# Part A of a gated mix: the order of transpositions, scores and normalizations between the projections

## The chip, the core and the metric

The kernel runs on one core of a Trainium2 chip. The metric is the device time of one execution in microseconds (us). Three executions of the kernel before took 1726.29, 1729.7 and 1736.17 us; the median is 1729.7 us. The profile is of a further execution, which took 1731.97 us.

## What is computed

Two attentions over the same 2048 rows of 640 are mixed by a gate per row. Attention A is recurrent: it goes through 64 segments of 32 rows, and each segment sees 8 memory rows that the segment before made. Attention B (a dilated window of 8 keys) has no recurrence.

```python
for s in range(64):                                   # A: H = 32 heads of Dh = 192, M = 8
    h = concat([mem, x[32*s : 32*s+32]])              # 40 rows
    q, k, v = h @ Wq, h @ Wk, h @ Wv                  # 640 -> 32*192 each
    scores = where(mask, q @ k.T * Dh**-0.5, -1e9)    # per head, 40 x 40
    o = (softmax(scores) @ v) @ Wo                    # 32*192 -> 640
    mem, out_a[s] = o[:8], o[8:]
g = sigmoid((x * gate_w).sum(-1))
return g * a + (1 - g) * b
```

## The kernel before, in words

Part B and a prepass come first (the first 380 us). The prepass also projects the last 8 rows of every segment's own x, since these need no recurrence, and packs the results in memory (`zpk_dram`), from where each segment loads its share: `load_z` (L709, keys and queries, 192 KB) and `load_vz` (L714, values, 96 KB). Part A, `part_a` (L684), is a loop over 64 segments. It fills the rest of the time, but for a last stage of some 60 us, `part_z`.

**A segment.** A projection's weights are 4 groups R of 8 heads. `m_qk(i, kcs)` (L725) projects queries (even i) or keys (odd i) of group R = i // 2; `m_v(R)` (L819) projects values. Such a projection has 5 steps kc, and each step has 4 matmuls of 32 weight columns by 384 columns, side by side on the four column strips of TensorE (tile position (0, 32 j)). In the following such four are called a quad, and this way of dividing the array is called the projections' tile mode. `c_qk(i)` (L738) copies the result from PSUM to a staging area of bf16 in SBUF (ScalarE, for i = 7 VectorE). `t_qk(i)` (L745) transposes it by three 128x128 matmuls against the identity into PSUM. `c_t(i)` (L755) copies the transposed rows on VectorE to where scores read them, for queries with a permutation (L758), for keys straight (L762). Scores are `s_a` (L775, the segment's own 32 keys: FULL is two matmuls with 128 rows, HALF two with 64 rows) and `s_b` (L787, the same against the prepass' keys). `e_exp(h)` (L795), four ScalarE activations, `e_mask(h)` (L801, VectorE) and `e_norm(h)` (L806) make the softmax of half h of the heads: two matmuls with a block of ones sum over keys (L810, L811), ScalarE makes the reciprocal by Ln and Exp (L814, L815), VectorE multiplies (L816, L817). `pv_half(h)` (L836) is 48 small matmuls with values, its results are copied (L861), `c_z` (L866) copies 8 more columns, and `o_group` (L884) is the output projection, 4 matmuls each, again in four column strips.

**The order.** Inside `part_a` the instructions of TensorE, ScalarE and VectorE are issued in the order in which the code is written (L907 to L986). The projections are interrupted by transpositions and scores, which use the array with 128 or 64 rows and 128 columns. I call such an interruption an excursion. The order before has five of them that hold transpositions or scores, and one more for `e_norm(1)`:

1. after m_qk(2): t_qk 0 and 1
2. after m_qk(4): t_qk 2 and 3, s_a(0)
3. after m_qk(6): s_a(1, FULL), s_b(0, FULL), t_qk 4 and 5, s_a(1, HALF), s_b(0, HALF)
4. after m_v(0): t_qk 6 and 7, s_a(2, FULL), e_norm(0), s_a(2, HALF)
5. after m_v(1): s_a(3), s_b(1)
6. within m_v(3): e_norm(1)

**Bytes.** Both areas, TZ and ZB, are shared by hand. Staging has two places (`assert i - 2 not in sts`, L740), so c_qk(i) waits until t_qk(i - 2) has read. Each transposition of a projection has a PSUM tile of its own from the pool `psx`, which has two buffers of one PSUM bank.

**Weights.** Of the 80 slices of weights (384 KB each) 66 stay in SBUF and 14 are streamed anew in every segment through five buffers (`wst`). `weights_setup` (L510) picks the 14 at even distances of an assumed timetable, in which `gap` gives the pauses between slices. DMAs for `wst` are issued on SP; those of `load_z`, `load_vz`, the next segment's x (L650), B's result `a4` (L954), the stores of results (L1001) and of the memory rows' part of the attention (L968) are issued on ScalarE's queue, in the order of the code.

Of the kernel before, what the change touches and what calls it, by code (L numbers as in the profile page):

```python
# [10 lines left out]
BF = mybir.dt.bfloat16  # L11
# [16 lines left out]
class _K:  # L28
# [481 lines left out]
    def weights_setup(self):  # L510
        nc, tc = self.nc, self.tc
        keys = self.slice_keys()
        gap = {("q", 0, 0): 300, ("k", 0, 1): 160, ("k", 0, 3): 70, ("k", 1, 0): 450, ("k", 2, 0): 850, ("k", 3, 0): 1050,
               ("v", 1, 0): 1000, ("v", 2, 0): 600, ("v", 3, 0): 570, ("v", 3, 3): 200, ("oa", 6): 1200}
        at, t = {}, 0
        for k in keys:
            t += gap.get(k, 0)
            at[k] = t
            t += 163
        self.stream_keys = set()  # L520
        for i in range(N_STREAM):
# [12 lines left out]
        self.wstream = self.ctx.enter_context(tc.tile_pool(name="wstream", bufs=WBUFS))  # L534
# [149 lines left out]
    def part_a(self):  # L684
# [4 lines left out]
        with ctx:  # L689
            pers = ctx.enter_context(tc.tile_pool(name="a_pers", bufs=1, reuse_waits="tile"))  # L690
            ZB = pers.tile([128, 1536 + 160], BF, name="ZB")
            KV, ZA = self.TZ[:, 0:1536], self.TZ[:, 1920:2528]
            Vz = ZA[:, 224:608]
            QTa = ZB[:, 384:1536].rearrange("p (b r c i) -> p b r c i", b=6, r=2, i=8)
            Es = [z[:, 0:224].rearrange("p (a f) -> p a f", a=2) for z in (ZA, ZB)]
            zst = ZA[:, 32:416]
            oTz = zst.rearrange("p (c q) -> p c q", q=8)
            whi = ZB[:, 768:768 + 640]
            KT = KV[:, 0:768].rearrange("p (c k) -> p c k", k=32)
            V = [KV[:, f0:f0 + 384] for f0 in (0, 768, 384, 1152)]  # L700
            oTxs = [v.rearrange("p (c q) -> p c q", q=32) for v in V]
            a4 = ZB[:, 1536:1696]
            KTz = self.TZ[:, 1536:1920].rearrange("p (c k) -> p c k", k=32)
# [18 lines left out]
            for s in range(nseg):  # L722
# [14 lines left out]

                def c_qk(i):  # L738

                    assert i - 2 not in sts  # L740
                    sts[i] = KV[:, 768 + 384 * (i % 2):1152 + 384 * (i % 2)]
                    cp = nc.vector.tensor_copy if i == 7 else nc.scalar.copy
                    cp(sts[i], pqs[i][:, 0:384])  # L743

                def t_qk(i):  # L745
                    R = i // 2
                    st = sts.pop(i)
                    pT = psx.tile([128, 1024], BF, tag="x", name="ps_qkT")
                    pT = pT[:, 0:384].rearrange("p (t j b i) -> p t j b i", t=3, j=4, i=8)
                    for t in range(3):  # L750
                        nc.tensor.transpose(pT[:, t, :, :, :].rearrange("p j b i -> p (j b i)"),  # L751
                                            st[:, 128 * t:128 * t + 128], self.ident[:])
                    pTs[i] = pT

                def c_t(i):  # L755
                    R, pT = i // 2, pTs.pop(i)
                    if i % 2 == 0:
                        nc.vector.tensor_copy(  # L758
                            q_blocks(R)[:, 1:5, :, :].rearrange("p b c i -> p c b i"),
                            pT.rearrange("p t j b i -> p (t j) b i"))  # L760
                    else:
                        nc.vector.tensor_copy(KV[:, 384 * (R % 2):384 * (R % 2) + 384],  # L762
                                              pT.rearrange("p t j b i -> p (t j b i)"))

                def q_blocks(R):
                    b0 = 1 - R // 2
# [8 lines left out]
                def s_a(R, chunks):  # L775
                    h, r = R // 2, R % 2
                    if h not in pSs:
                        pSs[h] = psS.tile([128, 2, 512], F32, tag="S", name="ps_S")
                    for t, par, k0, k1 in chunks:
                        c = 4 * t  # L780
                        nc.tensor.matmul(grid(h, par)[:, :, 0:80].rearrange("p j (b r i) -> p j b r i", r=2, i=8)[:, :, :, r, :],  # L781
                                         lhsT=KT[k0:k1, 12 * r + c:12 * r + c + 4, :],
                                         rhs=q_blocks(R)[k0:k1, :, c:c + 4, :].rearrange("p b c i -> p c b i"),
                                         start=(r == 0 and t != 1), stop=False, tile_position=(k0, 0),
                                         skip_group_check=True)
# [20 lines left out]
                def e_norm(h):  # L806
                    E = Es[h]
                    EA, EB = E[:, :, 0:80], E[:, :, 80:112]
                    pz = pSs[h][:, 0, 0:160].rearrange("p (a f) -> p a f", a=2)
                    nc.tensor.matmul(pz, lhsT=self.bones[:], rhs=EA, start=True, stop=False, skip_group_check=True)  # L810
                    nc.tensor.matmul(pz[:, :, 0:32], lhsT=self.bones[:], rhs=EB, start=False, stop=True,  # L811
                                     skip_group_check=True)
                    rz = pz
                    nc.scalar.activation(rz, pz, ACT.Ln)  # L814
                    nc.scalar.activation(rz, rz, ACT.Exp, scale=-1.0)  # L815
                    nc.vector.tensor_tensor(out=EA, in0=EA, in1=rz, op=ALU.mult)  # L816
                    nc.vector.tensor_tensor(out=EB, in0=EB, in1=rz[:, :, 0:32], op=ALU.mult)  # L817
# [95 lines left out]
                    tail()  # L913
                m_qk(0, (3, 4)); c_qk(0)
                m_qk(1, (3, 4)); c_qk(1)
                m_qk(2, range(KC))
                t_qk(0); c_t(0); c_qk(2); t_qk(1); c_t(1)
                m_qk(3, range(KC)); c_qk(3)
                if store is not None:
                    store()  # L920
                load_vz(s)
                m_qk(4, range(KC))
                if s == 0:
                    for load in self.last_loads:
                        load()
                t_qk(2); c_t(2); c_qk(4); t_qk(3); c_t(3)
                s_a(0, FULL); s_a(0, HALF)
                m_qk(5, range(KC)); c_qk(5)
                m_qk(6, range(KC))
                s_a(1, FULL); s_b(0, FULL)  # L930
                t_qk(4); c_qk(6); t_qk(5)
                s_a(1, HALF); s_b(0, HALF)
                c_t(4); c_t(5)
                e_exp(0)
                m_qk(7, range(KC)); c_qk(7)
                e_mask(0)
                m_v(0)
                t_qk(6); c_t(6); t_qk(7); c_t(7)
                s_a(2, FULL)
                e_norm(0)  # L940
                s_a(2, HALF)
                c_v(0)
                if s + 1 < nseg:
                    hT_next = self.load_seg(s + 1)
                else:
# [2 lines left out]
                    self.oz_free += [k for k in self.res_tiles if k[0] == "v"]  # L948
                    self.load_oz(0)
                m_v(1); c_v(1)  # L950
                for chunks in (FULL, HALF):
                    s_a(3, chunks)
                    s_b(1, chunks)
                nc.scalar.dma_start(a4[:], self.bsc_dram[32 * s:32 * s + 32, :].rearrange("t (j f) -> j t f", j=4))  # L954
# [162 lines left out]
```

## Time and profile before

| what | before |
|---|---|
| median of 3 runs | 1729.7 us |
| the profiled execution's time | 1731.97 us |
| its span in the profile | 1729.2 us |
| TensorE busy (matmuls; they overlap) | 1636.4 us, 95% |
| ScalarE, VectorE, GpSimd busy | 861.4 (50%), 632.3 (37%), 59.8 us (3%) |
| granted TensorE clock, mean | 0.99 |
| HBM traffic over the span | 275 GB/s |
| period of a segment in part A, mean of the 62 after the first | 20.42 us |
| the shortest period | 19.70 us (nine of the 62 read so) |

The profiled execution's time is 2.8 us over its span: what lies around the span. A period is the time between the first projection matmuls of two consecutive segments, read from the matmuls' starts in the trace. The chain of waits lists, back from the last instruction, what each step waited for; in part A it is nearly all TensorE work, and pieces called "issue" are times in which TensorE waited for nothing that the profile names.

### The profile page before, as it was taken

The numbers are of one execution on the slowest core, as the hardware profiler recorded it, in microseconds if no ns is written. First come the engines' busy times: TensorE is split into PE (matmuls) and PEld (weight loads), VectorE is DVE, ScalarE is ACT, GpSimd is POOL, SyncE is SP. The second block draws the span as 40 slices with busy tenths as digits, with TensorE's granted clock in tenths as the row PEclk, the third lists the DMA queues.
The fourth block names the chain that finished last, engine by engine and source line by source line (L and its number), as shares of the span: only waits on it lengthen the run. The fifth ranks groups of instructions, "written<-read, shape, count | busy, mean of one in ns | idle before, by whom it ended". The sixth has DMA issues, their size and how long they took to land.

```text
span 1729.2 us, 82024 instructions
## 1 busy us (share of the span) xinstructions
PE 1636.4 (95%) x36281; PEld 976.2 (56%) x36281; DVE 632.3 (37%) x2031; ACT 861.4 (50%) x2338; POOL 59.8 (3%) x124
## 2 busy tenths in 40 slices
PE   7887999899999999999999999999999999999989
PEld 4544544355555655555555555556555556555667
DVE  3665333233333333333333333333333333333330
ACT  3887322235555555555555455555555545555550
POOL 2030000000000000000000000000000000000000
PEclk9999899999999999999999999999999999999999
DMA  7898695989999999899888889989899999998991
GB/s 198 202 228 199 226 319 146 273 276 298 294 301 301 299 299 308 294 294 305 298 291 298 281 290 302 301 292 306 299 297 301 297 290 303 305 300 298 310 295 31
DMA packets 299696, 477.46 MB, mean 276 GB/s; under 512 B 100172, under 2 KB 176460, under 8 KB 299340
## 3 DMA queue, kind: packets, MB, share of 16 engines
q1 hardware_dynamic: 200208, 415.76, 74.2%
q10 hardware_dynamic: 99132, 56.46, 11.5%
q8 instruction: 283, 4.64, 1.1%
q14 instruction: 73, 0.60, 0.1%
HBM read 430.40 MB, written 44.48 MB: 275 GB/s over the span
## 4 chain that ended last, share of the span: by engine, by line
PE 85%; DMA 6%; ACT 3%; issue 3%; DVE 1%; ACTq 1%; SPq 1%; DVEq 0%
PE ps_qk L734 25%; PE ps_v L827 13%; PE ps_wo L891 12%; PE ps_pre L603 6%; PE ps_qkT L751 6%; PE ps_S L781 5%; PE ps_oT L850 3%; PE ps_z L1048 3%; PE ps_pre L617 3%; ACT ZB L975 2%; DMA bqkT<-bqk_dram 2%; PE ps_bqk L234 2%; PE ps_mem L901 1%; PE ps_S L790 1%; DMA OT<-bo_dram 1%
## 5 line engine op out<-in xcount | busy, mean ns | idle before, releaser
L743 ACT CAST TZ<-ps_qk 128x384 bf16<-128x384 f32 x448 | 208.3, 479 | 333.5 <-PE ps_qk L734 189.3
L734 PEld LDWEIGHTS <-hT 128*32 128x32 bf16 x10240 | 247.0, 96 | 158.7 <-issue 17.2
L758 DVE COPY ZB<-ps_qkT 128x384 bf16<-128x384 bf16 x256 | 91.6, 358 | 376.8 <-PE ps_qkT L751 210.5
L734 PE MATMUL ps_qk<-wres_q,hT 128*32 128x384 bf16 x4096 | 225.2, 327 | 2.1 <-issue 2.1
L827 PE MATMUL ps_v<-wlate_v,hT 128*32 128x384 bf16 x4096 | 224.0, 328 | 0.0
L734 PE MATMUL ps_qk<-wlate_k,hT 128*32 128x384 bf16 x3328 | 202.7, 328 | 1.8 <-issue 1.8
L891 PEld LDWEIGHTS <-TZ 128*32 128x32 bf16 x6144 | 154.8, 96 | 68.6 <-issue 20.2
L734 PE MATMUL ps_qk<-wst,hT 128*32 128x384 bf16 x1792 | 154.0, 328 | 1.8 <-issue 1.1
L827 PEld LDWEIGHTS <-hT 128*32 128x32 bf16 x5120 | 113.4, 96 | 67.1 <-issue 4.3
L891 PE MATMUL ps_wo<-wlate_oa,TZ 128*32 128x384 bf16 x2560 | 140.1, 327 | 2.9 <-issue 2.2
L781 PE MATMUL ps_S<-ZB,TZ 128*128 128x160 bf16 (+1 forms) x1024 | 136.4, 237 | 0.3 <-DMA ZB<-zpk_dram 0.3
L891 PE MATMUL ps_wo<-wlate_ob,TZ 128*32 128x256 bf16 x2688 | 124.0, 275 | 8.4 <-issue 7.2
L751 PE MATMUL ps_qkT<-ident,TZ 128*128 128x128 bf16 x1536 | 129.7, 220 | 0.4 <-ACT TZ L743 0.3
L751 PEld LDWEIGHTS <-TZ 128*128 128x128 bf16 x1536 | 89.0, 98 | 61.2 <-issue 40.6
L799 ACT ACTIVATE ZB<-ps_S 32x224 bf16<-32x224 f32 x256 | 89.0, 348 | 42.6 <-PE ps_S L790 38.6
L861 DVE CAST TZ<-ps_oT 128x192 bf16<-128x192 f32 x256 | 79.5, 351 | 63.7 <-PE ps_oT L855 63.5
L861 ACT CAST TZ<-ps_oT 128x192 bf16<-128x192 f32 x256 | 69.8, 327 | 58.3 <-PE ps_oT L855 58.3
L781 PEld LDWEIGHTS <-TZ 128*128 128x128 bf16 (+1 forms) x1024 | 58.8, 95 | 67.8 <-issue 40.4
L904 DVE CAST hT<-ps_mem 128x24 bf16<-128x24 f32 x126 | 22.5, 179 | 202.3 <-PE ps_mem L901 202.3
L834 ACT CAST TZ<-ps_v 128x384 bf16<-128x384 f32 x192 | 92.4, 481 | 3.2
L827 PE MATMUL ps_v<-wst,hT 128*32 128x384 bf16 x1024 | 86.7, 329 | 3.6 <-DMA wst<-in_A_Wv_dram 3.6
L799 ACT ACTIVATE TZ<-ps_S 32x224 bf16<-32x224 f32 x256 | 88.8, 347 | 2.3
(137 smaller groups left out, 2229.9 us busy)
## 6 DMA issues: line engine op xcount, KB each, us to landing
wst<-in_A_Wq_dram SPq DMA_DIRECT2D x260, 384.0 KB
wst<-in_A_Wv_dram SPq DMA_DIRECT2D x260, 384.0 KB
wst<-in_A_Wk_dram SPq DMA_DIRECT2D x195, 384.0 KB
wst<-wscr SPq DMA_DIRECT2D x192, 384.0 KB
zpk_dram<-ZS ACTq DMA_DIRECT2D x4, 3072.0 KB
ZB<-zpk_dram ACTq DMA_DIRECT2D x64, 192.0 KB
wres_q<-in_A_Wq_dram SPq DMA_DIRECT2D x16, 384.0 KB
wlate_v<-in_A_Wv_dram SPq DMA_DIRECT2D x16, 384.0 KB
```

What stands on the lines that cost most here:

```text
L603: nc.tensor.matmul(ps[:], lhsT=sls[r][kc][:, c0:c0 + 128], rhs=zTi[:, kc, :], start=(kc == 0), stop=(kc == KC - 1))
L617: mm = nc.tensor.matmul(pss[g][:], lhsT=zTi[:, kc, 128 * st:128 * st + 128], rhs=sls[kc][:, 512 * g:512 * g + 512], start=(kc == 0), stop= ...
L734: nc.tensor.matmul(pq[32 * j:32 * j + 32, 0:384], lhsT=hT[:, kc, :], rhs=sl[:, 384 * j:384 * j + 384], start=(kc == 0), stop=(kc == KC - 1 ...
L743: cp(sts[i], pqs[i][:, 0:384])
L751: nc.tensor.transpose(pT[:, t, :, :, :].rearrange("p j b i -> p (j b i)"), st[:, 128 * t:128 * t + 128], self.ident[:])
L758: nc.vector.tensor_copy(q_blocks(R)[:, 1:5, :, :].rearrange("p b c i -> p c b i"), pT.rearrange("p t j b i -> p (t j) b i"))
L781: nc.tensor.matmul(grid(h, par)[:, :, 0:80].rearrange("p j (b r i) -> p j b r i", r=2, i=8)[:, :, :, r, :], lhsT=KT[k0:k1, 12 * r + c:12 * ...
L799: nc.scalar.activation(E[ps], pSs[h][ps, :, 112 * j:112 * j + 112], ACT.Exp, scale=scale_a)
L827: nc.tensor.matmul(pvs[R][32 * j:32 * j + 32, 0:384], lhsT=hT[:, kc, :], rhs=sl[:, 384 * j:384 * j + 384], start=(kc == 0), stop=(kc == KC ...
L834: cp(V[R], pvs[R][:, 0:384])
L861: cps[j % 2](oTxs[2 * h + j // 2][:, 6 * (j % 2):6 * (j % 2) + 6, :], pos[j][:, 0:240].rearrange("p (c q) -> p c q", q=40)[:, :, 8:40])
L891: nc.tensor.matmul(pso[part][32 * jj:32 * jj + 32, 0:n], lhsT=oTxs[2 * (R // 2) + j // 2][:, 6 * (j % 2) + 3 * (R % 2) + t, :], rhs=o_weig ...
```

## The change

The order within a segment is rewritten so that there are three excursions with transpositions or scores:

1. after two of the five steps of m_qk(4): t_qk 0 to 3, with c_t 0 to 3 between them
2. after m_qk(7): s_a(0, FULL), s_a(1, FULL), s_b(0, FULL), t_qk 4 to 7, then the three HALF pairs; e_exp(0) and c_t 4 to 7 follow
3. after m_v(1): s_a(2, FULL), s_a(3, FULL), s_b(1, FULL), the sums of e_norm(0), then the three HALF pairs

`e_norm` is cut in two: the matmuls stay in `e_norm`, Ln, Exp and the multiplications become `e_recip`. The sums of half 1 are made by 8 matmuls of 32 columns in the projections' tile mode instead of 2 of 128 columns. Staging has four places. Transpositions i and i + 1 share one PSUM tile, half a bank each. The transposed keys of groups 0 and 1 go to places in ZB and TZ that are free at that time (`kt_runs`; those of group 1 in two copies, one of them where `a4` lies), those of groups 2 and 3 over staging places 2 and 3. The store of the last segment's result is issued before m_qk(2) instead of after m_qk(3), and the load of `a4` comes after e_recip(0). m_v(3) is cut 2 + 2 + 1 instead of 3 + 2. `gap` is given anew, which picks four other slices for streaming (k 1 3, q 2 2, q 3 0 and v 0 0 in place of k 1 0, q 2 4, k 2 2 and q 3 4).

```diff
-        gap = {("q", 0, 0): 300, ("k", 0, 1): 160, ("k", 0, 3): 70, ("k", 1, 0): 450, ("k", 2, 0): 850, ("k", 3, 0): 1050,
-               ("v", 1, 0): 1000, ("v", 2, 0): 600, ("v", 3, 0): 570, ("v", 3, 3): 200, ("oa", 6): 1200}
+        gap = {("q", 0, 0): 300, ("k", 0, 1): 160, ("k", 0, 3): 70, ("q", 2, 2): 900, ("v", 0, 0): 1900, ("v", 2, 0): 1100,
+               ("v", 3, 2): 600, ("v", 3, 4): 200, ("oa", 6): 1200}
...
+            kt_runs = lambda R: ([(0, 3, ZB[:, 0:384])], [(0, 2, self.TZ[:, 1920:2176]), (2, 3, ZB[:, 1536:1664])],
+                                 [(0, 3, V[2])], [(0, 3, V[3])])[R]
...
-                    sts[i] = KV[:, 768 + 384 * (i % 2):1152 + 384 * (i % 2)]
+                    sts[i] = V[i % 4]
...
-                    pT = psx.tile([128, 1024], BF, tag="x", name="ps_qkT")
-                    pT = pT[:, 0:384].rearrange("p (t j b i) -> p t j b i", t=3, j=4, i=8)
+                    if i % 2 == 0:
+                        pTs["two"] = psx.tile([128, 2, 512], BF, tag="x", name="ps_qkT")
+                    pT = pTs["two"][:, i % 2, 0:384].rearrange("p (t j b i) -> p t j b i", t=3, j=4, i=8)
...
-                        nc.vector.tensor_copy(KV[:, 384 * (R % 2):384 * (R % 2) + 384],
-                                              pT.rearrange("p t j b i -> p (t j b i)"))
+                        src = pT.rearrange("p t j b i -> p (t j b i)")
+                        for t0, t1, dst in kt_runs(R):
+                            nc.vector.tensor_copy(dst, src[:, 128 * t0:128 * t1])
...
-                    nc.tensor.matmul(pz, lhsT=self.bones[:], rhs=EA, start=True, stop=False, skip_group_check=True)
-                    nc.tensor.matmul(pz[:, :, 0:32], lhsT=self.bones[:], rhs=EB, start=False, stop=True,
-                                     skip_group_check=True)
+                    if h == 0:
+                        nc.tensor.matmul(pz, lhsT=self.bones[:], rhs=EA, start=True, stop=False, skip_group_check=True)
+                        nc.tensor.matmul(pz[:, :, 0:32], lhsT=self.bones[:], rhs=EB, start=False, stop=True,
+                                         skip_group_check=True)
+                    else:
+                        for x, E_x in ((80, EA), (32, EB)):
+                            for j in range(4):
+                                sl = slice(32 * j, 32 * j + 32)
+                                nc.tensor.matmul(pz[sl, :, 0:x], lhsT=self.bones[:, sl], rhs=E_x, start=(x == 80),
+                                                 stop=(x == 32), tile_position=(0, 32 * j), skip_group_check=True)
+
+                def e_recip(h):
...
-                m_qk(2, range(KC))
-                t_qk(0); c_t(0); c_qk(2); t_qk(1); c_t(1)
-                m_qk(3, range(KC)); c_qk(3)
                 if store is not None:
                     store()
+                m_qk(2, range(KC)); c_qk(2)
+                m_qk(3, range(KC)); c_qk(3)
                 load_vz(s)
-                m_qk(4, range(KC))
+                m_qk(4, (0, 1))
+                for i in range(4):
+                    t_qk(i); c_t(i)
+                m_qk(4, (2, 3, 4)); c_qk(4)
+                m_qk(5, range(KC)); c_qk(5)
...
-                t_qk(2); c_t(2); c_qk(4); t_qk(3); c_t(3)
-                s_a(0, FULL); s_a(0, HALF)
-                m_qk(5, range(KC)); c_qk(5)
-                m_qk(6, range(KC))
-                s_a(1, FULL); s_b(0, FULL)
-                t_qk(4); c_qk(6); t_qk(5)
-                s_a(1, HALF); s_b(0, HALF)
-                c_t(4); c_t(5)
+                m_qk(6, range(KC)); c_qk(6)
+                m_qk(7, range(KC)); c_qk(7)
+                s_a(0, FULL); s_a(1, FULL); s_b(0, FULL)
+                for i in range(4, 8):
+                    t_qk(i)
+                s_a(0, HALF); s_a(1, HALF); s_b(0, HALF)
                 e_exp(0)
-                m_qk(7, range(KC)); c_qk(7)
+                for i in range(4, 8):
+                    c_t(i)
                 e_mask(0)
-                m_v(0)
-                t_qk(6); c_t(6); t_qk(7); c_t(7)
-                s_a(2, FULL)
-                e_norm(0)
-                s_a(2, HALF)
-                c_v(0)
+                m_v(0); c_v(0)
...
-                for chunks in (FULL, HALF):
-                    s_a(3, chunks)
-                    s_b(1, chunks)
+                s_a(2, FULL); s_a(3, FULL); s_b(1, FULL); e_norm(0)
+                s_a(2, HALF); s_a(3, HALF); s_b(1, HALF)
+                e_recip(0)
                 nc.scalar.dma_start(a4[:], self.bsc_dram[32 * s:32 * s + 32, :].rearrange("t (j f) -> j t f", j=4))
                 e_exp(1)
                 e_mask(1)
                 m_v(2); c_v(2)
+                m_v(3, (0, 1))
                 pos = pv_half(0)
-                m_v(3, (0, 1, 2))
+                m_v(3, (2, 3))
                 c_z(0, pos, (1, 3), "dd")
-                e_norm(1)
-                m_v(3, (3, 4)); c_v(3)
+                e_norm(1); e_recip(1)
+                m_v(3, (4,)); c_v(3)
```

More of the change, by code (lines that the diff above doesn't have):

```diff
@@ L691, in part_a @@
             ZB = pers.tile([128, 1536 + 160], BF, name="ZB")
-            KV, ZA = self.TZ[:, 0:1536], self.TZ[:, 1920:2528]
-            Vz = ZA[:, 224:608]
+            V = [self.TZ[:, 384 * f:384 * f + 384] for f in range(4)]
+            KTz = self.TZ[:, 1536:1920].rearrange("p (c k) -> p c k", k=32)
+            E0, Vz, zst = self.TZ[:, 1920:2144], self.TZ[:, 2176:2560], self.TZ[:, 1984:2368]
             QTa = ZB[:, 384:1536].rearrange("p (b r c i) -> p b r c i", b=6, r=2, i=8)
-            Es = [z[:, 0:224].rearrange("p (a f) -> p a f", a=2) for z in (ZA, ZB)]
-            zst = ZA[:, 32:416]
+            Es = [z.rearrange("p (a f) -> p a f", a=2) for z in (E0, ZB[:, 0:224])]
             oTz = zst.rearrange("p (c q) -> p c q", q=8)
             whi = ZB[:, 768:768 + 640]
-            KT = KV[:, 0:768].rearrange("p (c k) -> p c k", k=32)
-            V = [KV[:, f0:f0 + 384] for f0 in (0, 768, 384, 1152)]
+            kt_runs = lambda R: ([(0, 3, ZB[:, 0:384])], [(0, 2, self.TZ[:, 1920:2176]), (2, 3, ZB[:, 1536:1664])],
+                                 [(0, 3, V[2])], [(0, 3, V[3])])[R]
+            KTs = [[z[:, f0:f0 + 128] for z, f0 in places] for places in (
+                [(ZB, 0), (ZB, 128), (ZB, 256)], [(self.TZ, 1920), (self.TZ, 2048), (ZB, 1536)],
+                [(V[2], 0), (V[2], 128), (V[2], 256)], [(V[3], 0), (V[3], 128), (V[3], 256)])]
             oTxs = [v.rearrange("p (c q) -> p c q", q=32) for v in V]
             a4 = ZB[:, 1536:1696]
-            KTz = self.TZ[:, 1536:1920].rearrange("p (c k) -> p c k", k=32)
             psm = ctx.enter_context(tc.tile_pool(name="psm", bufs=2, space=bass.MemoryType.PSUM, reuse_waits="tile"))
@@ L738, in c_qk @@
                 def c_qk(i):
-                    assert i - 2 not in sts
-                    sts[i] = KV[:, 768 + 384 * (i % 2):1152 + 384 * (i % 2)]
+                    assert i - 4 not in sts
+                    sts[i] = V[i % 4]
                     cp = nc.vector.tensor_copy if i == 7 else nc.scalar.copy
@@ L781, in s_a @@
                         nc.tensor.matmul(grid(h, par)[:, :, 0:80].rearrange("p j (b r i) -> p j b r i", r=2, i=8)[:, :, :, r, :],
[L782 removed]
+                                         lhsT=KTs[R][t][k0:k1, :],
                                          rhs=q_blocks(R)[k0:k1, :, c:c + 4, :].rearrange("p b c i -> p c b i"),
@@ L809, in e_norm @@
                     pz = pSs[h][:, 0, 0:160].rearrange("p (a f) -> p a f", a=2)
-                    nc.tensor.matmul(pz, lhsT=self.bones[:], rhs=EA, start=True, stop=False, skip_group_check=True)
-                    nc.tensor.matmul(pz[:, :, 0:32], lhsT=self.bones[:], rhs=EB, start=False, stop=True,
-                                     skip_group_check=True)
+                    if h == 0:
[9 more added lines that the diff above has]
+                def e_recip(h):
+                    E = Es[h]
+                    EA, EB = E[:, :, 0:80], E[:, :, 80:112]
+                    pz = pSs[h][:, 0, 0:160].rearrange("p (a f) -> p a f", a=2)
                     rz = pz
```

## The prediction

> **What bounds the kernel now.** I read the engines' shares, then the chain of waits for the whole span, then the chain and the timeline of single segments.
>
> ```profile
> PE 1636.4 (95%) x36281; PEld 976.2 (56%) x36281; DVE 632.3 (37%) x2031; ACT 861.4 (50%) x2338; POOL 59.8 (3%) x124
> ...
> PE 85%; DMA 6%; ACT 3%; issue 3%; DVE 1%; ACTq 1%; SPq 1%; DVEq 0%
> ```
>
> The end is set by TensorE, and in part A the chain is TensorE piece after piece. So a segment costs what TensorE's pieces cost, plus its waits. The chain of one segment (start, us, what):
>
> ```profile
> 916.00 0.44 PE ps_qkT L751 x6
> 916.44 1.74 PE ps_qk L734 x40
> 918.18 0.44 PE ps_qkT L751 x6
> 918.62 0.31 PE ps_S L781 x4
> 918.93 1.74 PE ps_qk L734 x40
> 920.67 0.24 PE ps_S L781 x2
> 920.91 0.11 PE ps_S L790 x2
> 921.02 0.34 PE ps_qkT L751 x6
> 921.36 0.17 PE ps_S L781 x2
> 921.53 0.06 PE ps_S L790 x2
> 921.59 0.93 PE ps_qk L734 x20
> 922.52 0.81 PE ps_v L827 x20
> ```
>
> Six transpositions take 0.44 us behind a projection and 0.34 within an excursion; twenty projection matmuls take 0.93 behind an excursion and 0.81 behind other projections. So going into an excursion costs 0.10 and coming back 0.12 us, and the step to 64 rows is in the 0.17 of the first HALF pair. Around the other engines the timeline shows what their steps take (start, us, engine, line):
>
> ```profile
> 935.83 0.51 PE L751 MATMUL ps_qkT<-ident,TZ 128*128 128x128 bf16 x6
> ...
> 936.27 0.36 DVE L758 COPY ZB<-ps_qkT 128x384 bf16<-128x384 bf16 x1 [1.51 <-PE ps_qkT L751]
> 936.55 0.35 DVE L762 COPY TZ<-ps_qkT 128x384 bf16<-128x384 bf16 x1
> ...
> 944.08 0.29 ACT L814 ACTIVATE ps_S<-ps_S 128x160 f32<-128x160 f32 x1 [1.02 <-PE ps_S L811]
> 944.40 0.29 ACT L815 ACTIVATE ps_S<-ps_S 128x160 f32<-128x160 f32 x1
> 944.91 0.56 ACTq L954 DMA_DIRECT2D ZB<-bsc_dram  x1
> 945.76 1.42 ACT L799 ACTIVATE ZB<-ps_S 32x224 bf16<-32x224 f32 x4 [0.57 <-PE ps_S L790]
> 947.29 0.28 DVE L803 TENSOR_TENSOR ZB<-ZB,mask 128x224 bf16<-128x224 bf16 x1 [1.60 <-ACT ZB L799]
> 947.62 0.23 PE L810 MATMUL ps_S<-ZB,bones 128*128 128x160 bf16 x1
> ```
>
> From a transposition's first matmul to its copy are 0.44 us, the copy takes 0.36, the next copy starts 0.28 after it, and from the end of a VectorE step (947.57) to TensorE's matmul behind it are 0.05.
>
> **What the change takes off TensorE**, in us per segment. Before, the excursions are 0.44; 0.44 + 0.31; 0.24 + 0.11 + 0.34 + 0.17 + 0.06; 0.85 and 0.59 (the fourth and fifth, the same way from the rows at 923.33 and 925.11), so 3.55. Five ways back at 0.12 are 0.60. e_norm(1) is 0.18 + 0.03, and the 8 matmuls behind it take 0.44 where 8/20 of 0.81 are 0.32: 0.33. Together 4.48. After: twelve transpositions, 0.44 + 0.34; second excursion 0.24 + 0.14 + 0.11 for the FULL pairs, 0.68 for the transpositions, 0.17 + 0.08 + 0.06 for the HALF pairs (0.08 for the pair that no row shows alone: one matmul of 0.07 with its neighbour beside it); third the same without transpositions, with 0.10 for e_norm(0); three ways back, 0.36; e_norm(1) as two quads of the lengths of L810 and L811, 0.07 + 0.03. Together 0.78 + 1.48 + 0.90 + 0.36 + 0.10 = 3.62. TensorE's own work falls by **0.86**, times 64 segments 55 us.
>
> **What it adds.** The order of the built kernel shows waits that the diff does not. In the first excursion t_qk(i) and c_t(i) are written alternately, and 0 and 1 (2 and 3) share a PSUM tile. The first matmul of t_qk(1), and that of t_qk(3), wait for VectorE: t_qk(1) for c_t(0), t_qk(3) for c_t(2), which stands behind c_t(1). TensorE runs in order, so the rest of m_qk(4) is behind them. From the first transposition: c_t(0) 0.44 to 0.80; t_qk(1) at 0.85; c_t(1) at 1.29; c_t(2) 1.57 to 1.93; t_qk(3) 1.98 to 2.15. Without the waits the twelve take 12/6 of 0.34, 0.67. **Lost: 1.48.** In the second excursion all transpositions come before the copies, and no such wait is there.
>
> The Trainium skill, "PSUM — Partial Sum Buffer", section "PSUM bank collisions raise a hardware error", says that TensorE must not write a bank while VectorE reads it in the same partitions, whatever the columns. By it this wait can't be dropped while two transpositions share a bank; no run here shows a collision. With the wait the sum is that above, without it 1.48 less.
>
> ScalarE is next. Ln and Exp of half 0 come behind the third excursion's sums and stand, with the issue of a4's load, before e_exp(1); in the timeline above they were over a projection earlier. From the second sum matmul: Ln at 0.29 (943.79 to 944.08), Exp at 0.61, the issue 0.09 behind it (as L650's at 944.49 behind 944.40) and 0.56 long: 1.26; four exponentials from 1.30 to 2.72, mask 2.83 to 3.11 (0.11 from 947.18 to 947.29), sums of half 1 at 3.16. TensorE has until then the HALF pairs (0.34 with the end of the sum), m_v(2) 0.93, two steps 0.32, pv_half(0) 0.48 (0.21, 0.05, 0.19, 0.03 in the chain), two steps 0.44: 2.51. **Lost: 0.6** (0.65 by the rows; I round down, as issues partly run beside the engine; if the load's issue does not hold e_exp(1) at all, 0.3).
>
> From the sums of half 1 to pv_half(1) the chain Ln, Exp, VectorE takes 1.69 (947.62 to the matmul at 949.31), ScalarE's copies of values among it. TensorE had about 1.6 of work there; now it has 0.10 + 0.16 + 0.97 + 0.12 = 1.35. **Lost: 0.3** (0.25 to 0.45, the higher if the first output groups wait for ScalarE's copies of pv_half(0), which now stand behind a later e_exp(1)).
>
> What I cost at nothing: one more copy on VectorE (c_t(3) in two), since VectorE has 1.5 us before c_qk(7); c_t(3)'s wait for the store of a4's bytes, which lands 3.9 us (median, by its packets) after an issue some 4.1 before the copy, and even at its longest, 6.0, ends before c_qk(7); m_qk(4) behind c_qk(2), which is free 0.1 us before; the 12 added instructions of 986; the streamed slices, which land 3.1 to 4.6 us after their issue, while the timetable has at least 5.98 us for five of them (6.63 before). If that cover failed it would be about 1 us per late slice.
>
> One wait that exists gets shorter. The mean period is 20.42, the shortest 19.70: 0.72 per segment go to gaps of up to 1.6 us that the chain calls issue. In the trace nearly all end 2.2 to 3.1 us after the start of a 16 KB packet of the instruction queue and are a multiple of 256 TensorE instructions apart: the next block of code is late. A segment has 3.9 such blocks, and the new waits lengthen one or two of them by 0.9 to 1.5 us, so some of these gaps close. Bounds: nothing, or 0.4. I take 0.17, a quarter, nearer to nothing since most gaps lie in the output projection, which stays as it is.
>
> **Sum.** −0.86 + 1.48 + 0.6 + 0.3 − 0.17 = +1.35 per segment, 64 segments: +86 us. On the profiled execution's 1732 this is 1818; that execution is 2.3 over the median, so 1815.
>
> **Rivals.**
>
> (1) The copies are not in the way, that is, the shared bank costs little because copies run beside the transpositions. Then −0.86 + 0.9 − 0.1: nothing is left of the gain, 1726. Against it: the waits in the built order. 3%.
>
> (2) It does what the pieces say: modes are changed less often, ScalarE's work is hidden by m_v(2) and pv_half(0). −0.86 × 64 = −55, 1675, the other side. It decides if both kinds of wait above are under 0.86 together; for it speaks that in the timeline the sums of half 1 start 0.05 after their mask without TensorE losing, against it that this leaves no slack. 4%.
>
> (3) c_t(1) writes where load_z put the keys, so it now waits for GpSimd's copy (L711), which is over 4.7 us after the segment's first matmul; c_t(1) is due at 5.4. The load lands 4.7 us after its issue (median), 5.6 in one of twenty, 6.6 at most. If contention makes 6 the rule, 0.27 more per segment: 1832. 6%.
>
> (4) The clock. The page of the profile shows a granted clock of 9 or more tenths in nearly every slice; here an excursion of 2.2 us has 0.67 us of matmuls in it. If the grant fell to half for the ten quads behind (1.62 us), it would cost 1.6 per segment, 1920. 2%. The Trainium skill, "TensorE: Matmul & The Clock Gate", section "Part 4: PE-mode transpose", says that transpositions do not count as work for the clock in the same way; by that rule this case comes out. Six in a row do no harm to the projections behind them in the trace (1.74 for 40, of which 0.12 are the way back).
>
> The forecast has 85%. The range takes in the bounds: waits together 2.0 to 2.6, the gaps 0 to 0.4, so from +0.77 (1779) to +1.72 (1840); I take 1785 to 1840, which also holds rival 3 and leaves out rivals 1, 2 and 4. A measurement of this kernel can tell about 0.5% from no change; faster by more: 4%, within: 3%, slower: 93%.
>
> **What would show it.** Right: mean period near 21.8; in the chain the first excursion as six and six transpositions broken by VectorE's copies (2.2 us in all), its second and third excursion 1.5 and 0.9; a wait of TensorE for the mask of half 1 of 0.5 to 0.6, and ScalarE as what ends the wait before pv_half(1); fewer pieces "issue". Wrong: twelve transpositions in 0.8 us, or sums of half 1 without a wait, or DMA of wst as what TensorE waits for.

## The result, and the profile after

The changed kernel takes **1817.86 us** (median of 4 runs, 1816.19 to 1827.33) against 1727.99 us (1720.36 to 1736.17) for the kernel before on the same chip: ratio 1.053, 95% interval 1.047 to 1.059. It is slower, by 90 us where 85 were forecast. The profiled execution took 1816.19 us with a span of 1814.4.

The lines of the page that answer to the first two shown of before, the engines' shares and the chain by engine:

```profile
PE 1621.8 (89%) x36665; PEld 1008.2 (56%) x36665; DVE 647.3 (36%) x2095; ACT 867.6 (48%) x2338; POOL 60.1 (3%) x124
...
PE 68%; ACT 12%; DMA 6%; DVE 5%; issue 5%; ACTq 2%; SPq 1%; DVEq 0%; POOL 0%; POOLq 0%
```

TensorE is busy 15 us less, and yet the span is 85 us longer: TensorE's share of the chain falls from 85 to 68%, ScalarE's rises from 3 to 12%, VectorE's from 1 to 5%. "issue" rises as well, since the chain now has many steps of 0.02 to 0.05 us from one engine to the next, which are counted there.

The chain of waits of one segment after (start, us, what), first and second excursion:

```profile
972.57 0.29 PE ps_qkT L754 x3
...
972.95 0.37 DVE ZB L761
...
973.36 0.34 PE ps_qkT L754 x3
...
973.78 0.15 DVE ZB L767
...
974.05 0.36 DVE ZB L761
...
974.46 0.33 PE ps_qkT L754 x3
974.78 3.05 PE ps_qk L736 x72
977.83 0.38 PE ps_S L785 x4
978.21 0.11 PE ps_S L794 x2
978.33 0.67 PE ps_qkT L754 x12
```

In the first excursion (972.57 to 974.78, 2.21 us) the chain leaves TensorE for VectorE's copies twice, ahead of t_qk(1) and of t_qk(3). In the second, where no copy stands between, the same twelve transpositions take 0.67 us.

The same view, from the last sum of half 0 to pv_half(1):

```profile
981.60 0.04 PE ps_S L816
...
981.73 0.30 ACT ps_S L830
...
982.04 0.02 ACT ps_S L831
...
982.11 0.56 ACTq L967
...
982.79 0.13 ACT ZB L803
...
984.25 0.28 DVE ZB L807
...
984.57 0.28 PE ps_S L822 x8
```

Here the chain runs through ScalarE: Ln, the rest of Exp, then 0.56 us for the issue of a4's load (L967), and only then the exponentials of half 1 (L803). What TensorE itself waited for over part A, from the list of waits (us in total, times, longest us):

```profile
PE ps_qkT L754 <- DVE ZB L761: 72.2, 126, 0.9
PE ps_S L822 <- DVE ZB L807: 31.1, 63, 0.8
PE ps_wo L907 <- issue: 11.7, 18, 1.2
```

The first two rows are two waits that the change adds, twice and once per segment. The same list of before has no row of the first kind, and of the second:

```profile
PE ps_S L810 <- DVE ZB L803: 0.5, 2, 0.3
```

The timeline of after shows the second wait within a segment (start, us, engine, line):

```profile
983.58 0.35 PE L843 MATMUL ps_v<-wlate_v,hT 128*32 128x384 bf16 x4
983.75 0.34 PE L843 MATMUL ps_v<-wst,hT 128*32 128x384 bf16 x4
984.57 0.28 PE L822 MATMUL ps_S<-ZB,bones 128*32 128x160 bf16 x8 [0.49 <-DVE ZB L807]
```

One quad starts 0.17 us after the other, but the sums of half 1 start 0.82 after the last quad: 0.65 us are lost there.

The mean period of the 62 segments goes from 20.42 to 21.76 (+1.34), the shortest from 19.70 to 21.25 (+1.55). Shortest periods are free of the gaps that the prediction put down to late blocks of code; the difference of mean and shortest is then about what the gaps cost, 0.72 before and 0.51 after.

### The profile page after: what moved, and what is told of

The parts are those of the page before. It is cut to its first block, busy times and chain, and to the rows that moved or that the text cites. A ratio compares the mean times of both kernels' runs of the same rounds, so it can differ in the third digit from the quotient of the medians.

```text
span 1814.4 us, 82536 instructions
## 1 busy us (share of the span) xinstructions
PE 1621.8 (89%) x36665; PEld 1008.2 (56%) x36665; DVE 647.3 (36%) x2095; ACT 867.6 (48%) x2338; POOL 60.1 (3%) x124
## 4 chain that ended last, share of the span: by engine, by line
PE 68%; ACT 12%; DMA 6%; DVE 5%; issue 5%; ACTq 2%; SPq 1%; DVEq 0%; POOL 0%; POOLq 0%
PE ps_qk L736 23%; PE ps_wo L907 8%; PE ps_v L843 7%; PE ps_pre L603 6%; PE ps_qkT L754 6%; ACT ZB L803 4%; PE ps_S L785 3%; PE ps_z L1062 3%; PE ps_pre L617 3%; DVE ZB L761 2%; ACT ps_S L830 2%; ACTq L967 2%; PE ps_oT L866 2%; PE ps_bqk L234 2%; ACT ZB L989 2%
## 5 line engine op out<-in xcount | busy, mean ns | idle before, releaser
L736 PEld LDWEIGHTS <-hT 128*32 128x32 bf16 x10240 | 265.2, 96 | 144.3 <-DVE hT L920 13.2
L736 PE MATMUL ps_qk<-wres_q,hT 128*32 128x384 bf16 x4096 | 236.4, 327 | 0.6 <-issue 0.4
L736 PE MATMUL ps_qk<-wlate_k,hT 128*32 128x384 bf16 x3584 | 212.3, 326 | 0.3 <-ACT TZ L745 0.3
L843 PEld LDWEIGHTS <-hT 128*32 128x32 bf16 x5120 | 120.2, 96 | 67.4 <-issue 4.4
L754 PEld LDWEIGHTS <-TZ 128*128 128x128 bf16 x1536 | 93.6, 97 | 109.1 <-issue 109.1
L803 ACT ACTIVATE TZ<-ps_S 32x224 bf16<-32x224 f32 x256 | 89.0, 348 | 113.6 <-PE ps_S L794 111.4
L736 PE MATMUL ps_qk<-wst,hT 128*32 128x384 bf16 x1536 | 132.2, 329 | 0.8 <-issue 0.5
L843 PE MATMUL ps_v<-wst,hT 128*32 128x384 bf16 x1280 | 108.2, 328 | 3.6 <-DMA wst<-in_A_Wv_dram 3.6
L803 ACT ACTIVATE ZB<-ps_S 32x224 bf16<-32x224 f32 x256 | 89.0, 348 | 32.4 <-DVE TZ L832 27.2
L745 DVE CAST TZ<-ps_qk 128x384 bf16<-128x384 f32 x64 | 35.7, 558 | 146.8 <-PE ps_qk L736 146.8
L713 POOL COPY TZ<-ZB 128x384 bf16<-128x384 bf16 x64 | 32.5, 507 | 1582.2 <-DMA ZB<-zpk_dram 766.9
```

Source lines behind the costliest of these rows:

```text
L736: nc.tensor.matmul(pq[32 * j:32 * j + 32, 0:384], lhsT=hT[:, kc, :], rhs=sl[:, 384 * j:384 * j + 384], start=(kc == 0), stop=(kc == KC - 1 ...
L803: nc.scalar.activation(E[ps], pSs[h][ps, :, 112 * j:112 * j + 112], ACT.Exp, scale=scale_a)
L843: nc.tensor.matmul(pvs[R][32 * j:32 * j + 32, 0:384], lhsT=hT[:, kc, :], rhs=sl[:, 384 * j:384 * j + 384], start=(kc == 0), stop=(kc == KC ...
```

## The experiments

Each run stands beside runs of the kernel before on the same chip; ratios are to these, with 95% intervals. "Shortest" and "mean" are periods, read as before. "Late blocks" counts, over part A, the places where TensorE enters a new block of 256 instructions more than 0.43 us after its last matmul started, and sums what is over the usual 0.16. Before: 47 of 239, 37 us. After: 33 of 227, 23 us. (The totals are the entries found in a trace; the 62 periods hold 239 in the order before and 242 in that after.) Periods and blocks are those of the one traced execution of each kernel, times are medians of several.

### Undoing one wait at a time

**copies_last**: all transpositions of the first excursion ahead of their copies.

```diff
                 for i in range(4):
-                    t_qk(i); c_t(i)
+                    t_qk(i)
+                for i in range(4):
+                    c_t(i)
```

> The changed kernel with one edit: in the first excursion all four transpositions are written first and the four copies behind them, so that no transposition waits for VectorE. My theory (TensorE waits for the copies of the bank it shares with them, 1.45 us per segment): first excursion 0.8 us in place of 2.2, period down by 1.45 before gaps for code; some of those gaps come back (0.1 to 0.2), so about 1.3 x 64 = 83 us less than the changed kernel, 1730 to 1742, as fast as before within 1%. Rival (the waits are idle time that the chain would spend anyway on ScalarE or weights): 1800 or more. Rival (the changes of mode saved are all gain once the waits are gone): 1675.

1757.56 us (1747.5 to 1761.17), ratio 1.017 (1.013 to 1.021). The shortest period falls by 1.44, to 19.81: the wait is worth what the prediction said (1.48). But the mean is 20.76: late blocks rise from 23 to 43 us. So the time missed the expected range by 16 us, on the side of the gaps.

**own_tiles**: in the first excursion each transposition has a PSUM tile, so a bank, of its own.

```diff
-                    if i % 2 == 0:
+                    if i % 2 == 0 or i < 4:
```

> The changed kernel with one edit: in the first excursion each transposition has a PSUM tile of its own (two buffers), transpositions and copies still alternate. Theory: 0 and 1 run through, 2 waits for the copy of 0 and 3 for the copy of 1, since there are two buffers: transpositions end 1.3 us after the first in place of 2.15, so 0.8 to 0.85 per segment less, some 50 us: 1760 to 1775. Rival (any copy between transpositions holds TensorE, bank or not): no change from 1818. Rival (sharing alone was the matter): as fast as with the copies behind, 1735.

1792.15 us (1788.19 to 1795.53), ratio 1.038 (1.035 to 1.041); shortest 20.43 (−0.82, as expected), mean 21.27, late blocks 37 us. The time missed the expected range by 17 us, again on the side of the gaps. t_qk(1) no longer waits for c_t(0); with two buffers t_qk(2) and t_qk(3) still do wait. So giving each transposition a tile of its own removes 0.82 of the lost 1.44, and putting the copies last removes all of it with the tiles still shared.

**a4_late**: the load of a4 issued behind e_exp(1).

```diff
                 e_recip(0)
-                nc.scalar.dma_start(a4[:], ...)
                 e_exp(1)
+                nc.scalar.dma_start(a4[:], ...)
```

> The changed kernel with one edit: the load of a4 is issued behind e_exp(1) and no longer ahead of it. Theory: the issue (0.56 us) holds the exponentials of half 1 back, and through them the sums of half 1: TensorE's wait there falls from about 0.55 to 0.2 to 0.3, and some of it comes back before pv_half(1). 0.15 to 0.3 per segment, 8 to 18 us less: 1800 to 1810. Rival (the issue runs beside the engine and holds nothing): no change, 1818.

1813.53 us (1808.88 to 1819.87), ratio 1.050 (1.046 to 1.053). The shortest period falls by 0.54, to 20.71, so nearly the whole 0.56 of the issue was on the path, more than the 0.15 to 0.3 expected. But the time is 4 us over the expected range, and its ratio can't be told from that of the changed kernel (1.053, 1.047 to 1.059). In the trace the mean even rises, 21.76 to 21.88: late blocks go from 23 to 52 us and take the gain back. That trace is of the slowest of its four executions (1819.87), that of the changed kernel of its fastest, so the 52 us are an upper end.

**both_edits**: copies_last and a4_late together.

> The changed kernel with both edits, copies behind the transpositions and a4's load behind e_exp(1). Theory: both add, as they are at different places of the segment: period before code gaps 19.5 (19.7 before the change), mean about 20.2, 1712 to 1722. Rival (TensorE's gaps for code take back what is won): 1728, as before.

1758.54 us (1742.14 to 1764.7), ratio 1.017 (1.011 to 1.022). The shortest period is 19.27, below the 19.70 of before, as the sum of the pieces asks. The mean is 20.88; 61 of 238 blocks are late, 73 us. The expected 1712 to 1722 was wrong: I had taken the gaps for a fixed tax. The time is that of copies_last alone (1757.56), though the shortest period is 0.54 less. What TensorE waited for in both_edits:

```profile
PE ps_wo L907 <- issue: 32.4, 31, 2.6
PE ps_oT L866 <- issue: 14.6, 13, 2.1
PE ps_oT L871 <- issue: 12.4, 8, 2.3
```

Of waits for VectorE 0.2 us are left in this list; all three rows are gaps without a named cause, in pv_half and the output projection. Before has 10.5, 3.8 and 3.9 us in these.

### Are the gaps made by the streamed weights?

**before_no_stream**, **both_no_stream**, **after_no_stream**: the three orders with nothing streamed in part A.

```diff
         if key in self.ahead:
             return self.ahead.pop(key)
+        if self.part_a_runs:
+            if len(self.kept) < WBUFS:
+                t = self.wstream.tile([128, 1536], BF, name="wst", tag="wst")
+                self.load_slice(self.wstream, key, "wst", "wst", t)
+                self.kept.append(t)
+            self.n_kept += 1
+            return self.slice_view(key, self.kept[self.n_kept % len(self.kept)])
```

> The kernel before, with the 14 streamed slices of every segment replaced by five that are loaded once at the start of part A and used in turn (so wrong weights stand in their place; all instructions of TensorE, ScalarE and VectorE stay). Theory: the gaps called issue, at multiples of 256 TensorE instructions, are blocks of code that come late because they share the DMA engines with the streamed slices. Then they nearly vanish: the mean period falls from 20.4 to 19.7-19.9, the shortest stays 19.7, and the time falls by 64 x 0.5 to 0.7, to 1682-1695. Rival: the blocks are late by themselves, whatever else the engines carry; then about 1726, as before.

> The kernel of both_edits, with the streamed slices replaced in the same way. Theory: its late blocks of code cost it 73 us (mean period 20.9 where the shortest is 19.3) and are what keeps it slower than the kernel before. Without streaming the mean falls to 19.3-19.5, so the time falls by 64 x 1.4 to 1.6, to 1656-1669, and it is faster than the kernel before with the same replacement by 64 x 0.4, some 20-28 us. Rival: another loss hides in it; then the two differ as they do with streaming, it being about 30 us the slower.

> The changed kernel, with the streamed slices replaced by five that are loaded once, as in before_no_stream (wrong weights stand in their place, all instructions of the engines stay). Theory: its waits for VectorE and ScalarE, 1.55 per segment by the shortest periods (21.25 against 19.70), do not come from DMA. Then all periods are near 21.2, and the time is that of before_no_stream, 1680, plus 64 x 1.4 to 1.55: 1770-1780. Rival: part of these waits comes from transfers (the load of a4, GpSimd's copy of the keys, slices); then under 1760.

| order | time, us | ratio to before | mean period | shortest | late blocks |
|---|---|---|---|---|---|
| before_no_stream | 1680.21 | 0.974 (0.971 to 0.977) | 19.71 | 19.70 | 0 of 248 |
| both_no_stream | 1658.65 | 0.961 (0.958 to 0.964) | 19.33 | 19.27 | 3 of 256 |
| after_no_stream | 1783.64 | 1.037 (1.034 to 1.039) | 21.32 | 21.26 | 1 of 231 |

The shortest periods stay where they were, and the means come down to them. (before_no_stream came out 2 us under its expected range.) A line of each page, for before_no_stream the HBM traffic (before: 275 GB/s), for both_no_stream the chain by engine:

```profile
HBM read 80.83 MB, written 44.48 MB: 75 GB/s over the span
```

```profile
PE 84%; ACT 8%; DMA 4%; DVE 1%; issue 1%; ACTq 1%; SPq 1%; DVEq 0%
```

The 8% of ScalarE in the second are its steps ahead of pv_half(1), for which TensorE still waits in this order.

From TensorE's entry into a block to the start of the next 16 KB packet of the instruction queue the trace has 1.76 us (median) in before and 0.37 in before_no_stream. And when each step of TensorE is compared with the same step of the order without streams, 43 of the 49 us that the 62 periods of before lose lie at entries into a block, and 86 of the 103 us of both_edits. So the code's packets start late because of the streamed slices' traffic, and the gaps are blocks of code that come late through it; this is now shown. Where the two meet, in the DMA engines or at the memory behind them, no run separates. The order of both_edits is the faster one without streams, by 22 us. after_no_stream is 103 us over before_no_stream (4 us more than the upper end expected): the waits that the change adds do not come from the streamed slices. The smaller transfers, such as a4's load, stay in all three.

### What a change of tile mode costs

**before_six**: the kernel before with one excursion more.

```diff
-                m_qk(2, range(KC))
-                t_qk(0); c_t(0); c_qk(2); t_qk(1); c_t(1)
+                m_qk(2, (0, 1, 2, 3))
+                t_qk(0); c_t(0)
+                m_qk(2, (4,)); c_qk(2)
+                t_qk(1); c_t(1)
```

> The kernel before with the first transposition taken one step earlier, with the last step of m_qk(2) between it and the second: one excursion more, no other work. Theory of the prediction's first part: a way into an excursion costs 0.10 and the way back 0.12 us, so +0.22 per segment, +14, about 1740, with a shortest period of 19.9. Rival: changes of tile mode cost next to nothing here, since other waits cover them; then 1724-1730.

1741.19 us (1736.02 to 1742.48), ratio 1.0085 (1.0056 to 1.0115); the shortest period is 19.92, +0.22. So the sum of the two prices read from the chain (0.10 in, 0.12 back) holds.

### Can the gain be kept with streaming?

**before_pv_first**: pv_half(0) taken from between m_v(2) and m_v(3) to ahead of m_v(2), and the first c_z to ahead of m_v(3).

```diff
                 e_exp(1)
+                pos = pv_half(0)
                 e_mask(1)
                 m_v(2); c_v(2)
-                pos = pv_half(0)
-                m_v(3, (0, 1, 2))
                 c_z(0, pos, (1, 3), "dd")
+                m_v(3, (0, 1, 2))
```

> The kernel before with pv_half(0) behind the fifth excursion, ahead of m_v(2) and the first three steps of m_v(3) instead of between them and c_z: the dense stretch before pv_half(1) is cut by longer steps. Theory of late code blocks: the same work, so the shortest period stays at 19.7, but fewer blocks are late, mean period 20.2-20.3, the time 1714-1722. Rivals: no difference, 1724-1730; or ScalarE's copies of pv_half(0), now ahead of Ln and Exp of half 1, delay pv_half(1), some 0.3 per segment, 1745.

1723.12 us (1715.09 to 1735.59), ratio 0.9985 (0.9963 to 1.0008): no difference that can be told. In its one trace the mean period is 20.26 and 43 of 240 blocks are late (29 us), a hint in the expected direction and no more.

**both_lull** and **best_lull**: other slices are streamed (the second with three edits more).

```diff
-        for i in range(N_STREAM):
-            left = [k for k in keys if k not in self.stream_keys]
-            self.stream_keys.add(min(left, key=lambda k: abs(at[k] - (i + 0.5) * t / N_STREAM)))
+        self.stream_keys |= {("q", 0, 1), ("q", 1, 0), ("k", 1, 2), ("q", 2, 2), ("k", 2, 1), ("q", 3, 1), ("k", 3, 2), ("v", 0, 0),
+                             ("v", 0, 3), ("v", 1, 2), ("v", 3, 3), ("oa", 5), ("oa", 7), ("ob", 4)}
```

> both_edits with other slices streamed, nothing else: two of the streamed value slices (v 1 4, v 2 4) give way to v 1 2 and k 2 1, and six others move by a step or two, so that no streamed slice is used between 10.7 and 13.9 us of a segment, and fewer transfers start in the 3 us behind it. Theory: in both_edits the blocks of code that come late are those asked for 12 to 16 us into the segment, when the DMA engines move 300 to 345 KB per us (before: 250 to 310); with room there the lost 73 us fall to 30-45, the time from 1758 to 1720-1735. Rival: the engines are full anyhow, and what is taken from one place queues at another: 1745-1765.

The further edits of best_lull:

```diff
+                nc.scalar.dma_start(a4[:], ...)
                 m_v(1); c_v(1)
-                s_a(2, FULL); s_a(3, FULL); s_b(1, FULL); e_norm(0)
+                s_a(2, FULL); e_norm(0); s_a(3, FULL); s_b(1, FULL)
...
                 e_exp(1)
-                nc.scalar.dma_start(a4[:], ...)
...
-                c_z(0, pos, (0, 2), "aa")
+                c_z(0, pos, (0, 2), "dd")
```

> both_lull with three more edits: the load of a4 goes to the place of the next segment's x, e_norm(0) stands directly behind s_a(2, FULL), and c_z's first copy of half 0 goes from ScalarE to VectorE. By the waits that these shorten the shortest period is 19.0-19.15 (19.27 in both_edits). If the room in the stream holds, the time is 1708-1725, faster than the kernel before; if denser code only makes more blocks late, 1740-1755, slower.

1768.44 us (1763.86 to 1774.24), ratio 1.028 (1.025 to 1.031), and 1771.4 us (1762.91 to 1776.81), 1.029 (1.025 to 1.033). In both_lull late blocks did fall as expected, 73 to 43 us, but a new wait took their place:

```profile
PE ps_v L842 <- DMA wst<-in_A_Wv_dram: 21.6, 40, 2.3
```

Slices now come late, v 1 2 in 42 of the segments and v 0 3 in 16: both are used only 5.0 us after their buffer comes free. In best_lull the same slices are late, and 57 of 234 blocks (56 us), so it tells nothing of its three other edits. Both times are over even the slower range that was expected: neither theory nor rivals had the late slices.

**both_13**: both_edits with one streamed slice less, and one buffer less to hold it for good.

```diff
-N_STREAM = 14
+N_STREAM = 13
...
-WBUFS = 5
+WBUFS = 4
...
-        for i in range(N_STREAM):
-            left = [k for k in keys if k not in self.stream_keys]
-            self.stream_keys.add(min(left, key=lambda k: abs(at[k] - (i + 0.5) * t / N_STREAM)))
+        self.stream_keys |= {("q", 0, 2), ("k", 0, 3), ("k", 1, 2), ("q", 2, 2), ("q", 3, 0), ("k", 3, 4), ("v", 0, 0), ("v", 1, 3),
+                             ("v", 2, 0), ("v", 3, 3), ("oa", 3), ("ob", 0), ("ob", 4)}
```

> both_edits with 13 streamed slices and four buffers for them in place of 14 and five (the freed buffer holds one slice more for good), picked so that four uses are always at least 5.7 us apart. 384 KB less per segment move, and they are spread evenly. Theory: blocks of code come late because the DMA engines are nearly full, so less traffic makes fewer of them late without making slices late (in both_lull slices with 5.0 us were late, one with 5.4 in few segments): the lost 73 us fall to 30-50, the time from 1758 to 1715-1740. Rivals: four buffers are too few and slices come late by 0.5 us or more per segment, 1760-1790; or the engines stay as full, 1745-1760.

**1702.91 us** (1694.15 to 1707.97), ratio 0.987 (0.984 to 0.990): 1.3% under the kernel before, a small gain, but clear of the spread. It also lies 12 us under the expected range. Its waits:

```profile
PE ps_wo L906 <- issue: 13.0, 18, 1.7
PE ps_oT L870 <- issue: 5.5, 7, 2.0
...
PE ps_v L842 <- DMA wst<-in_A_Wv_dram: 2.9, 4, 1.8
...
PE ps_oT L865 <- issue: 2.2, 4, 0.8
```

The gaps are back to about the size of before (35 of 247 blocks, 30 us), slices of all kinds are late eight times, 3.9 us in all, the shortest period is 19.27 and the mean 19.93. Less traffic (405 MB read, both_edits 430), with the slices picked anew, did what moving the same traffic in both_lull did not. How much of the 20 us belongs to the new order and how much to the smaller stream stays open: the old order with 13 slices was not run, and both_13 differs from both_edits in the number of slices and in which they are.

## Why the prediction was right, point by point

Without streams every period is nearly the same, so TensorE's time can be divided among steps without the gaps (each matmul counted from its start to the next start, medians over the segments). That gives the prediction's terms one by one, per segment, after_no_stream and both_no_stream against before_no_stream:

| step | predicted | measured |
|---|---|---|
| TensorE's own work | −0.86 | −0.86 |
| first excursion waits for the copies | +1.48 | +1.44 (transposition lines 1.54 to 2.98) |
| sums of half 1 wait for the mask | +0.6 | +0.66 (they start 0.82 after the last quad, a step is 0.15) |
| before pv_half(1) | +0.3 | +0.33 (0.15 ahead of the first output group, 0.18 from there to pv_half(1)) |
| sum of these | +1.52 | +1.57 |
| fewer gaps | −0.17 | −0.21 (0.72 to 0.51) |
| change of the mean period | +1.35 | +1.34 |

The first row of the last column is what is left of the sum: 1.57 − 1.44 − 0.66 − 0.33. (The sum is of medians; the shortest periods differ by 1.55.)

**TensorE's own work.** Right. Scores fell by 0.40 (1.79 to 1.39), the sums of both halves by 0.09, the projections, whose lines hold most ways into and out of excursions, by 0.34 without the waits; the transpositions themselves cost as before (1.56 to 1.54). The durations of the excursions came out (2.21 against 2.2, 1.47 against 1.48, 0.89 against 0.90, the last from the starts at 980.97 and 981.86 in the timeline), and before_six confirms the price of a change of mode. One trap lies here: the lines of the value projection grow by only 0.57 (3.74 to 4.31), since in before they also hold the way into e_norm(1), which the changed order no longer has. Whoever takes the 0.57 for the whole wait finds that TensorE's work fell by 0.1 too little.

**The shared tile.** Right in mechanism and size: copies_last took away 1.44, own_tiles 0.82. The Trainium skill, "PSUM — Partial Sum Buffer", section "PSUM bank collisions raise a hardware error", asks for such a wait where two transpositions share a bank. own_tiles shows only that with a bank of its own t_qk(1) does not wait, and no run here shows a collision.

**ScalarE's chain.** Right: a4_late shows 0.54 of it to be the issue of one load. The 0.65 of the rows was nearer than the 0.6 to which I rounded it down. In every segment of before, after and a4_late the sums of half 1 start 0.05 us after the mask ends; with the load out of the way 0.10 of the wait is left. Before pv_half(1) it was the higher case of the prediction: in every segment the first output group waits for ScalarE's copy of pv_half(0).

**Costed at nothing.** The streamed slices were on time (one wait of 1.7 us in part A), with the bound I gave (5.98 us of lead). In both_lull slices with 5.0 us of lead do come late. c_t(3) waited for the store of a4's bytes 41 times, 20.8 us in all, but no wait of TensorE follows from it in the list.

**The gaps.** Their sign and their cause (late blocks) were right. That the size came out is in part luck: a quarter of the gaps was a choice between bounds, and no row gave the quarter itself. What I missed is how elastic they are: I asked how many of them longer waits would close, and priced a quarter. For the experiments the same question in reverse was the larger one, since shortening a wait by 0.54 to 1.44 us gave back 20 us (copies_last) or up to 29 us (a4_late) in gaps. My expectations of copies_last, own_tiles, a4_late and both_edits failed there.

**The rivals.** (1) copies not in the way and (2) pieces only: excluded by the chain. What (2) says of the pieces is half true: with both waits gone the shortest period is 0.43 under that of before, not 0.86, because the wait before pv_half(1) (0.33) and 0.10 of that for the mask stay. (3) load_z late: its load stands once in the whole chain of part A (6.01 us long), as in before (7.16), so it is not the rule. (4) the clock: the granted clock is 0.99 in both kernels. The first excursion holds transpositions alone, over 2.2 us, and the eighteen quads behind it in the chain (L736, 974.78 to 977.83, 72 matmuls in 3.05 us) run at the usual pace: 0.12 for the way back and 0.163 for each. The rule of the Trainium skill ("TensorE: Matmul & The Clock Gate", section "Part 4: PE-mode transpose"), that transpositions do not count as work for the clock in the same way, cost nothing here.

## What to carry to other kernels

Merging interruptions of a TensorE stream saves a fixed price each (here 0.22 us), but it also puts consumer and producer next to each other: before counting the saving, look for every pair in the merged stretch that shares a buffer or a queue, DMA issues among them. Where TensorE has many small instructions and DMA is nearly full, compare shortest periods and means apart: a shorter wait shows in the first at once, and in the second only if the instruction blocks come in time. Here one streamed slice less helped, and the same traffic at other times did not.

## What the runs showed of the hardware

The profile lists the fetching of code as a DMA queue of its own; in part A it brings one packet of 16 KB for every 256 TensorE instructions. With 275 GB/s of traffic 47 of 239 blocks were late, 37 us of 1732; with the streams gone (part A's slices of the page at 28 to 35 GB/s) none of 248, and the kernel before became 45 us faster. The same instructions lose more when they follow more closely: a segment of both_edits issues the 998 instructions of after in 19.3 instead of 21.25 us, and its late blocks cost 73 us instead of 23. Density alone does not set the loss, though: a4_late, at 20.71 us, lost 52 us in its trace, copies_last, at 19.81, 43. The Trainium skill, "Runtime: NRT & Kernel Launch", section "Instruction fetch mechanics", calls the crossing of such a boundary mostly hidden. That agrees with the runs without streams; with streams the measurement decides, and it is not hidden.
